# An FNet and GeGLU block on one core: chunk sums, weight chunks, first loads and last splits of the down projection moved in the instruction order

## The chip, the cores and the metric

The kernel runs on one core of one Trainium2 chip. The metric is the device time of one execution in microseconds (us), lower is better. Before the change it is 743.65 us, the median of 3 runs (743.02 to 745.65). The engines of the core are PE (TensorE, matrix products), DVE (VectorE), ACT (ScalarE), POOL (GpSimd) and SP (SyncE, which here only issues DMAs). Each engine, and SP's queue of DMAs, takes its instructions strictly in the order in which the program gives them.

## The reference

```python
def A(x, seq_re, seq_im, hid_re, hid_im):        # Fourier mixing as matrix products
    a = x @ hid_re.T ; b = x @ hid_im.T          # (2048, 448)
    return seq_re @ a - seq_im @ b
def B(x, w_gate, w_up, w_down):                  # GeGLU, 448 -> 1792 -> 448
    return (gelu_tanh(x @ w_gate) * (x @ w_up)) @ w_down
h  = x + A(layernorm(x), ...)
h2 = h + B(layernorm(h), ...)                    # float32 in and out, 2048 rows
```

## The kernel before

All products run on PE in float16, each operand split into a high half (`hi_part`, an ACT copy) and a low half (`lo_part`, a DVE subtraction), so that three products of halves give nearly float32. GeGLU's three products use Strassen-like forms: seven products of sums of blocks in place of eight. The sums of the down projection's operand are made on POOL, and one small one on DVE.

The order of every engine is written out by hand (`manual_schedule`); a step waits only for the data and buffers that it names.

**DFT.** Steps n = 0 to 63 (`N_STEPS`) multiply sequence blocks. Beside them DVE and ACT split the blocks (`seq_hi`, `seq_lo`) and some of the 14 gate/up weight chunks: class `Weights` loads a chunk's raw form (two DMAs, tile `gu_raw`), makes its sums (`sums`, four DVE operations into `gu_s`), its halves (`split`, into `gu_w`), and stores it to DRAM (`w_dram`). Table `DFT_F` says which chunk is done at which step: six chunks; the other eight (`JIT_F`, chunks 3 to 10) are done during the next stage, two units ahead of their use.

**Gate and up, first block of rows.** Units t = 0 to 13, one chunk of 128 hidden columns each, 512 rows wide. A unit is a `GateUp` with PE steps x1, z1, y1, x2, z2, y2, y3, where x1 and z1 of unit t+1 stand before y1 of unit t+1 and y3 of unit t. Step y2 ends in a DVE write to tile `hs`, `c_last` in a GELU on ACT and a product on POOL, y3 in a second DVE write to `hs`; then `hs` is stored to DRAM (`hid_dram`). The same units prepare the seven down-weight chunks n (`down_sums` on POOL, `down_hi`, `down_lo`), two of them in unit 0, then one a unit (`PREPS`). After units 0 and 1 come the last two hidden-DFT products (`hid_mm(7, 0)`, `hid_mm(7, 1)`), both into one PSUM bank of pool `ps_tr`, and added to the residual on DVE (`hid_add`).

**Gate and up, other blocks, with the down projection.** Units t = 14 to 41, half as wide. In each unit one or two chunks d of the down projection run too (`COUNT`, 42 chunks; `dn_mm`, 21 matmuls each). A chunk is loaded from `hid_dram` (`hid_load`), summed (`dn_sums`), split (`dn_hi`, `dn_lo`) and multiplied. Every seventh chunk ends a row block p: `Drain` adds its products to the residual, on DVE from PSUM, and on POOL in 8 operations spread over the two units that follow. Chunks of the last two row blocks (d = 42 to 55, `LAST`) can only be multiplied at the end; `EARLY` says in which unit (30 to 41) the first twelve are prepared, straight from tile `hs`, in the unit after it is complete.

**Tail.** `prev.y3()` of unit 41, then chunks 42 to 55 on PE, with the last two chunks' splits, the drains and the stores.

Of the kernel before, what the change touches and what calls it, by code (L numbers as in the profile page):

```python
# [13 lines left out]
P = 128  # L14
# [18 lines left out]
def kernel(  # L33
# [673 lines left out]
    def hid_mm(p, g):  # L707

        y = ys[p, g] = ps_tr.tile([P, 512], F32, tag="tr", name=f"y_{p}_{g}")
        for k in range(7):  # L710
            for m, (lz, lw) in enumerate(((0, 0), (0, 1), (1, 0))):
                PE.matmul(  # L712
                    y[:, :D],
                    z[p][:, lz, k, g * P : (g + 1) * P],
                    wh[:, lw, k, :],
                    start=k == 0 and m == 0,
                    stop=k == 6 and m == 2,
                )
# [10 lines left out]
    DFT_F = ((13, 20), (12, 25), (11, 30), (0, 45), (1, 48), (2, 50))  # L729
    JIT_F = range(3, 11)  # L730
# [286 lines left out]
    def plus(dst, ps, other):  # L1017
# [4 lines left out]
        (b, n): dram.tile([P, 4 - 2 * b, 4, P], F32, name=f"hid_dram{b}_{n}") for b in range(2) for n in range(NC)  # L1022
    }

    class GateUp:
# [78 lines left out]
        def store(self):  # L1104

            k, n = divmod(self.f, NC)
            if self.block == 0:
                nc.sync.dma_start(
                    hid_dram[0, n][:, :, 2 * k : 2 * k + 2], hs[self.t].rearrange("p (n g) t -> p n g t", g=2)
                )  # L1110
            else:
                nc.sync.dma_start(hid_dram[1, n], hs[self.t].rearrange("p (n k) t -> p n k t", k=4))
# [8 lines left out]
    def hid_load(d):  # L1121
        p, n = divmod(d, NC)
        hid_in[d] = fpool.tile([P, 4, P], F32, tag="hid", bufs=4, name=f"hid{d}")
        nc.sync.dma_start(hid_in[d], hid_dram[p // 4, n][:, p % 4])

    def dn_hid(d):
        p, n = divmod(d, NC)
        if d in hid_in:
            return hid_in[d]
        return hs[2 * NF + 2 * n].rearrange("p (n k) t -> p n k t", k=4)[:, p % 2]  # L1130

    LAST = range(6 * NC, 8 * NC)
    EARLY = {2 * NF + 2 * n + 2 + k: (6 + k) * NC + n for n in range(6) for k in range(2)}

    def dn_places():
# [29 lines left out]
    def dn_sums(d):  # L1165
        t = dn_hid(d)
        if d in LAST:
            s = prep.tile([P, 5, P], F32, tag="s", name=f"dn_s{d}")
        else:
            s = late.tile([P, 5, P], F32, tag="dn_s", bufs=2, name=f"dn_s{d}")  # L1170
        dn_s[d] = s
        G.tensor_add(s[:, 0:2], t[:, 0:2], t[:, 2:4])  # L1172
        G.tensor_sub(s[:, 2:4], t[:, 1:4:2], t[:, 0:4:2])  # L1173
        V.tensor_add(s[:, 4], t[:, 0], t[:, 3])
# [100 lines left out]
    PREPS = {0: (0, 1), 1: (2,), 2: (3,), 3: (4,), 4: (5,), 5: (6,)}  # L1275
# [7 lines left out]
    for t in range(NF):  # L1283
# [13 lines left out]
        if t == NF - 1:  # L1297
            dn_sums(0)
# [27 lines left out]
        for n in PREPS.get(t, ()):  # L1326
            if n == 1:
                down_hi(n, 0)
                down_lo(n, 0)
            down_hi(n, 1)  # L1330
            for part in W_LO1:
                down_lo(n, 1, part)
            if n + 1 < NC:
                down_sums(n + 1)
# [27 lines left out]
        for n in PREPS.get(t, ()):  # L1362
            if 2 <= n and n + 2 < NC:
                down_load(n + 2)
# [11 lines left out]
    for t in range(NF, N_GU):  # L1376
# [4 lines left out]
        for d in steps.get(t + 2, []):  # L1381
# [8 lines left out]
        for d in ahead:  # L1390
            dn_sums(d)
# [29 lines left out]
        for d in ahead[1:]:  # L1421
            dn_lo(d)
        if extra is not None:
            dn_sums(extra)
# [5 lines left out]
        if NF < t <= 2 * NF and t % 2 == 0:  # L1430
# [104 lines left out]
```

## Time and profile before

| what | value |
|---|---|
| median of 3 runs (lowest to highest) | 743.65 us (743.02 to 745.65) |
| the profiled execution's own time | 745.72 us |
| its span, first to last instruction | 743.9 us |
| mean granted clock of TensorE | 0.991 |
| DVE busy | 519.4 us, 70% of the span |
| ACT busy | 354.7 us, 48% |
| POOL busy | 201.6 us, 27%, nearly all of it after 343 us |
| bytes moved by DMA | 149.46 MB |

The page sums each engine's busy time over the whole span. The stages differ in what limits them, so such sums say little by themselves: idle time of PE is to be looked for by place, in the timeline and the list of waits, where a row's square bracket gives the idle time ahead of it and the instruction whose end released it.

### The profile page before, as it was taken

The page shows a single profiled execution, that of the slowest core. Times are in us where ns is not written, and L with a number is a line of the kernel's source. Part 1 is how long each engine was busy: PE and PEld are TensorE (multiplying, and loading weights), DVE is VectorE, ACT ScalarE, POOL GpSimd, SP SyncE. Part 2 cuts the span into 40 slices and gives each one's busy share as a digit, 9 for nine tenths or more (in the row PEclk, how much of TensorE's full clock was granted, in tenths as well). Part 3 has the DMA queues.
Part 4 walks back from the last instruction along what each step waited for, and adds up shares of the span by engine and source line. Part 5 has one row for each costly group of instructions (what it writes and reads, how often), then busy time and mean ns, then how long its engine had stood idle before and what let it go on. Part 6 is the DMA issues. An engine that isn't in the chain of part 4 may idle for free.

```text
span 743.9 us, 13045 instructions
## 1 busy us (share of the span) xinstructions
PE 712.6 (96%) x4952; PEld 482.1 (65%) x4952; DVE 519.4 (70%) x1024; ACT 354.7 (48%) x656; POOL 201.6 (27%) x240
## 2 busy tenths in 40 slices
PE   9999999999999999999889799979999999989898
PEld 5555555555555557986334344449999999878788
DVE  7996546668356699996659995337767667878742
ACT  5875424254234355443437674435555545546430
POOL 0000000000000000001424312134474767787852
PEclk9999999999999999999999999989999999999999
DMA  7796729898949898455438688976797975646202
GB/s 260 253 241 196 189 26 293 151 324 183 270 121 251 179 250 267 126 140 155 133 118 282 226 273 208 221 239 193 224 308 257 270 248 178 219 167 208 112 1 75
DMA packets 112863, 149.46 MB, mean 201 GB/s; under 512 B 61600, under 2 KB 80160, under 8 KB 112800
## 3 DMA queue, kind: packets, MB, share of 16 engines
q1 hardware_dynamic: 112800, 148.63, 69.0%
q8 instruction: 38, 0.62, 0.4%
q14 instruction: 25, 0.20, 0.1%
HBM read 103.51 MB, written 31.20 MB: 181 GB/s over the span
## 4 chain that ended last, share of the span: by engine, by line
PE 31%; DVE 7%; POOL 5%; ACT 3%; issue 2%; DMA 2%; SPq 0%; DVEq 0%; ACTq 0%; POOLq 0%
PE acc_d L1214 11%; PE pY L1008 9%; PE pZ L1008 5%; PE pX L1008 5%; DVE gu_w L114 2%; POOL dn_s L1173 1%; POOL dn_s L1172 1%; POOL hr L970 1%; PE y L712 1%; POOL hs L1102 1%; ACT dn_w L108 1%; DVE dn_w L112 1%; DVE wd L114 1%; DMA hid<-hid_dram 1%; DMA gu_raw<-in_w_gu_dram 1%
## 5 line engine op out<-in xcount | busy, mean ns | idle before, releaser
L647 PE MATMUL acc<-xs,ws 128*128 128x448 f16 x1248 | 238.0, 352 | 0.0
L647 PEld LDWEIGHTS <-ws 128*128 128x128 f16 x1248 | 122.0, 98 | 114.1 <-DVE ws L114 0.2
L1008 PEld LDWEIGHTS <-gw 128*128 128x128 f16 x1209 | 118.9, 98 | 39.2 <-issue 14.7
L1214 PE MATMUL acc_d<-wd,dn_w 128*128 128x224 f16 x945 | 106.6, 260 | 1.5 <-DVE dn_w L112 1.2
L219 POOL TENSOR_TENSOR wd_s<-wd 128x448 f32<-128x448 f32 x7 | 8.2, 1171 | 355.3 <-DVE r_h L141 341.9
L1214 PEld LDWEIGHTS <-dn_w 128*128 128x128 f16 x945 | 91.1, 98 | 4.8 <-DVE dn_w L112 1.7
L1102 POOL TENSOR_TENSOR hs<-hs,c 128x256 f32<-128x256 f32 (+1 forms) x42 | 48.1, 1146 | 148.1 <-ACT c L1100 105.2
L1008 PE MATMUL pY<-hops,gw 128*128 128x256 f16 (+1 forms) x527 | 75.5, 287 | 8.0 <-ACT pY L1053 5.5
L1008 PEld LDWEIGHTS <-gu_w 128*128 128x128 f16 x429 | 42.1, 98 | 62.6 <-issue 14.1
L114 DVE SCALAR_TENSOR_TENSOR ws<-wr,ws 128x1024 f16<-128x1024 f32 (+2 forms) x66 | 75.0, 1141 | 10.3 <-ACT ws L108 10.3
L108 ACT ACTIVATE ws<-wr 128x1024 f16<-128x1024 f32 (+2 forms) x66 | 64.0, 981 | 24.8 <-DMA wr<-in_w_seq_dram 24.1
L712 PE MATMUL y<-wh,z 128*128 128x448 f16 x336 | 67.8, 359 | 2.4 <-DVE hx L722 2.4
L712 PEld LDWEIGHTS <-z 128*128 128x128 f16 x336 | 33.3, 99 | 33.8 <-issue 4.8
L1008 PE MATMUL pZ<-hops,gw 128*128 128x256 f16 (+1 forms) x341 | 50.9, 283 | 3.4 <-DVE c L1018 3.4
L112 DVE TENSOR_TENSOR dn_w<-dn_s,dn_w 128x640 f16<-128x640 f32 x45 | 45.9, 1020 | 8.6 <-ACT dn_w L108 8.5
L1008 PE MATMUL pX<-hops,gw 128*128 128x256 f16 (+1 forms) x341 | 51.4, 285 | 0.0
L1008 PE MATMUL pY<-hops,gu_w 128*128 128x512 f16 x187 | 44.7, 382 | 6.9 <-DVE hs L1018 5.9
L108 ACT ACTIVATE dn_w<-dn_s 128x640 f16<-128x640 f32 x45 | 33.0, 733 | 35.7 <-POOL dn_s L1173 25.7
L519 PEld LDWEIGHTS <-ws 128*128 128x128 f16 x504 | 48.3, 98 | 0.9
L1018 DVE SCALAR_TENSOR_TENSOR c<-pZ,u 128x256 f32<-128x256 f32 (+1 forms) x42 | 21.4, 509 | 34.5 <-PE pZ L1008 34.5
L1064 ACT ACTIVATE u<-pY 128x256 f32<-128x256 f32 (+1 forms) x42 | 18.9, 450 | 50.6 <-PE pY L1008 50.6
L970 POOL TENSOR_TENSOR hr<-hr,v 128x224 f32<-128x224 f32 x56 | 41.5, 767 | 1.7 <-ACT v L938 1.2
(156 smaller groups left out, 975.8 us busy)
## 6 DMA issues: line engine op xcount, KB each, us to landing
gw<-w_dram SPq DMA_DIRECT2D x31, 896.0 KB, 5.0
wr<-in_w_seq_dram SPq DMA_DIRECT2D x100, 256.0 KB, 4.7
w_dram<-gu_w SPq DMA_DIRECT2D x14, 896.0 KB, 5.0
gu_raw<-in_w_gu_dram SPq DMA_DIRECT2D x28, 384.0 KB, 5.8
hid_dram<-hs SPq DMA_DIRECT2D x21, 512.0 KB, 6.7
hid<-hid_dram SPq DMA_DIRECT2D x42, 256.0 KB, 5.7
wr<-in_w_seq_dram SPq DMA_DIRECT2D x14, 512.0 KB, 5.7
x<-in_x_dram SPq DMA_DIRECT2D x16, 224.0 KB, 4.3
```

Of the source, the lines that this page charges most:

```text
L108: A.activation(dst, src, AF.Copy, scale=scale)
L112: V.tensor_sub(dst, src, hi)
L114: V.scalar_tensor_tensor(dst, src, scale, hi, op0=ALU.mult, op1=ALU.subtract)
L519: PE.matmul(fast_sum(n, k), fast_a(n, i, lw, a), fast_b(j, lx, b), start=j == 0 and m == 0 and k % 2 == 0, stop=j == NT // 2 - 1 and m == ...
L647: PE.matmul(acc[key][:, :D], w[:, lw, block * P : (block + 1) * P], xs[c][:, lx, :], start=c == 0 and m == 0, stop=c == NT - 1 and m == 2,)
L712: PE.matmul(y[:, :D], z[p][:, lz, k, g * P : (g + 1) * P], wh[:, lw, k, :], start=k == 0 and m == 0, stop=k == 6 and m == 2,)
L970: op(x, x, m)
L1008: PE.matmul(ps, w[:, wl, wa + ws, :], ops[:, m + ms, :], start=first and n == 0, stop=last and n == len(terms) - 1, skip_group_check=True,)
L1018: V.scalar_tensor_tensor(dst, ps, SC, other, op0=ALU.mult, op1=ALU.add)
L1064: A.activation(self.u2, self.Y, AF.Copy, scale=SC)
L1102: G.tensor_mul(c22, c22, self.cols(self.c12))
L1214: PE.matmul(ps, w[:, la, a, :], wd[n][:, lb, b, :], start=n == 0 and m == 0 and opens, stop=n == NC - 1 and m == 2, skip_group_check=True,)
```

## The change

The function `dn_sums` for the chunks of unit t+2 moves from the head of unit t+1 to the end of unit t, and the loads and sums of `EARLY` chunks to one unit ahead of their halves. These chunks are now loaded from DRAM like the others, so that `hs` of the last block is stored too, and the ring of `hs` shrinks from 3 to 2 while that of `hid` grows from 4 to 6. `EARLY` keeps eight chunks; six are split in the tail. Four weight chunks (7 to 10) go from `JIT_F` to `DFT_F`, and three keep their place in the DFT in other steps. Chunks 0 to 2 of the down projection are loaded in unit 12 instead of 13. Down-weight chunk n is prepared wholly in unit n. `hid_mm(7, 1)` writes another PSUM bank.

```diff
 def hid_mm(p, g):
-    y = ys[p, g] = ps_tr.tile([P, 512], F32, tag="tr", name=f"y_{p}_{g}")
+    pool, tag = (ps_dn, "a3") if p == NP - 1 and g else (ps_tr, "tr")
+    y = ys[p, g] = pool.tile([P, 512], F32, tag=tag, name=f"y_{p}_{g}")
...
-DFT_F = ((13, 20), (12, 25), (11, 30), (0, 45), (1, 48), (2, 50))
-JIT_F = range(3, 11)
+DFT_F = ((13, 17), (12, 20), (11, 25), (10, 29), (9, 33), (8, 37), (7, 41), (0, 45), (1, 48), (2, 50))
+JIT_F = range(3, 7)
...
-            hs[self.t] = fpool.tile([P, 8, P], F32, tag="hs", bufs=3, name=f"hs_{self.name}")
+            hs[self.t] = fpool.tile([P, 8, P], F32, tag="hs", bufs=2, name=f"hs_{self.name}")
...
 def hid_load(d):
     p, n = divmod(d, NC)
-    hid_in[d] = fpool.tile([P, 4, P], F32, tag="hid", bufs=4, name=f"hid{d}")
-    nc.sync.dma_start(hid_in[d], hid_dram[p // 4, n][:, p % 4])
+    hid_in[d] = fpool.tile([P, 4, P], F32, tag="hid", bufs=6, name=f"hid{d}")
+    b = max(p // 2 - 1, 0)
+    nc.sync.dma_start(hid_in[d], hid_dram[b, n][:, p % 2 if b else p])
 def dn_hid(d):
-    if d in hid_in:
-        return hid_in[d]
-    return hs[2 * NF + 2 * n].rearrange("p (n k) t -> p n k t", k=4)[:, p % 2]
+    return hid_in[d]
-EARLY = {2 * NF + 2 * n + 2 + k: (6 + k) * NC + n for n in range(6) for k in range(2)}
+EARLY = dict(zip((32, 33, 35, 37, 38, 39, 40, 41), (42, 49, 43, 50, 44, 51, 45, 52)))
...
-PREPS = {0: (0, 1), 1: (2,), 2: (3,), 3: (4,), 4: (5,), 5: (6,)}
 for t in range(NF):
...
-        if t + 1 == NF:
+        if t + 2 == NF:
             for d in (0, 1, 2):
                 hid_load(d)
+        if t + 1 == NF:
             hr_load(0)
...
-        if t == NF - 1:
-            dn_sums(0)
         cur.y1()
...
-        for n in PREPS[t][:1] if t in PREPS else ():
-            down_hi(n, 0)
-            down_lo(n, 0)
+        if t < NC:
+            down_hi(t, 0)
+            down_lo(t, 0)
         cur.x2()
+        if t < NC:
+            down_hi(t, 1)
...
+        if t == NF - 2:
+            dn_sums(0)
+        if t == NF - 1:
+            dn_sums(1)
+            dn_sums(2)
...
 for t in range(NF, N_GU):
-        for d in steps.get(t + 2, []):
+        far = steps.get(t + 2, []) + ([EARLY[t + 1]] if t + 1 in EARLY else [])
+        far += [46] if t + 1 == N_GU else []
+        for d in far:
             hid_load(d)
...
         prev.y3()
-        for d in ahead:
-            dn_sums(d)
         cur.y1()
...
         for d in ahead[1:]:
             dn_lo(d)
+        for d in far:
+            dn_sums(d)
         if extra is not None:
-            dn_sums(extra)
             dn_hi(extra)
             dn_lo(extra)
         do(t, 3)
-        if NF < t <= 2 * NF and t % 2 == 0:
+        if NF < t and t % 2 == 0:
             before.store()
...
 prev.y3()
-dn_sums(48)
+hid_load(47)
+prev.store()
+jit = [46, 47, 48, 53, 54, 55]
 for i, d in enumerate(range(6 * NC, 7 * NC + 4)):
     dn_mm(d)
-    if i == 0:
-        dn_hi(48)
-        dn_lo(48)
-        dn_sums(55)
-        dn_hi(55)
-        dn_lo(55)
-    if i == 1:
+    if jit:
+        n = jit.pop(0)
+        dn_hi(n)
+        if jit:
+            dn_sums(jit[0])
+        dn_lo(n)
+        if len(jit) > 1:
+            hid_load(jit[1])
+    if i == 5:
         drain.sums(range(8))
         dn_store(5)
```

**SP, units 12 and 13** (`gw` is the weight chunk of two units later, `hid` a chunk of the down projection, `hops` the transposed rows of the next block). Before:

```order
L1116 DMA gw_4723<-w_dram_149 128x3584
L1108 DMA hid_dram_4_3682<-hs_4691 512x1x256
L305 DMA_TRANSPOSE hops_3923<-xs_1_4633 128x8x128
L305 DMA_TRANSPOSE hops_3923<-xs_1_4633 128x6x128
L305 DMA_TRANSPOSE hops_3923<-xs_1_4633 128x3x128
L1116 DMA gw_4788<-w_dram_156 128x3584
L1124 DMA hid_4790<-hid_dram_0_3678 128x512
L1124 DMA hid_4792<-hid_dram_1_3679 128x512
L1124 DMA hid_4794<-hid_dram_2_3680 128x512
L1225 DMA hr_4796<-h_dram_141 128x896
```

Now:

```order
L1117 DMA gw_4738<-w_dram_149 128x3584
L1126 DMA hid_4740<-hid_dram_0_3750 128x512
L1126 DMA hid_4742<-hid_dram_1_3751 128x512
L1126 DMA hid_4744<-hid_dram_2_3752 128x512
L1109 DMA hid_dram_4_3754<-hs_4706 512x1x256
L305 DMA_TRANSPOSE hops_3993<-xs_1_4648 128x8x128
L305 DMA_TRANSPOSE hops_3993<-xs_1_4648 128x6x128
L305 DMA_TRANSPOSE hops_3993<-xs_1_4648 128x3x128
L1117 DMA gw_4813<-w_dram_156 128x3584
L1224 DMA hr_4815<-h_dram_141 128x896
```

The three loads stand ahead of the three last transposes and of the store of unit 11, where they stood behind them.

**POOL, end of unit 38 to unit 39** (`dn_s` with a chunk's number are its sums, `hr4` the residual of row block 4 in its drain, `hs` with `c12` the product of `c_last`). Before:

```order
L1102 TENSOR_TENSOR hs_38_7674<-hs_38_7674,c12_38_7672 128x2x128
L1172 TENSOR_TENSOR dn_s46_7725<-hs_36_7430 128x256
L1173 TENSOR_TENSOR dn_s46_7725<-hs_36_7430 128x256
L970 TENSOR_TENSOR hr4_6917<-hr4_6917,v0_4_7570 128x224 x2
L970 TENSOR_TENSOR hr4_6917<-hr4_6917,v1_4_7571 128x224 x2
L1172 TENSOR_TENSOR dn_s38_7756<-hid38_7608 128x256
L1173 TENSOR_TENSOR dn_s38_7756<-hid38_7608 128x256
L1172 TENSOR_TENSOR dn_s39_7760<-hid39_7610 128x256
L1173 TENSOR_TENSOR dn_s39_7760<-hid39_7610 128x256
L1102 TENSOR_TENSOR hs_38_7674<-hs_38_7674,c12_39_7797 128x2x128
```

Now:

```order
L1103 TENSOR_TENSOR hs_38_7667<-hs_38_7667,c12_38_7665 128x2x128
L1171 TENSOR_TENSOR dn_s38_7718<-hid38_7603 128x256
L1172 TENSOR_TENSOR dn_s38_7718<-hid38_7603 128x256
L1171 TENSOR_TENSOR dn_s38_7718<-hid39_7605 128x256
L1172 TENSOR_TENSOR dn_s38_7718<-hid39_7605 128x256
L1171 TENSOR_TENSOR dn_s51_7725<-hid51_7607 128x256
L1172 TENSOR_TENSOR dn_s51_7725<-hid51_7607 128x256
L971 TENSOR_TENSOR hr4_6922<-hr4_6922,v0_4_7560 128x224 x2
L971 TENSOR_TENSOR hr4_6922<-hr4_6922,v1_4_7561 128x224 x2
L1103 TENSOR_TENSOR hs_38_7667<-hs_38_7667,c12_39_7791 128x2x128
```

The sums of the chunks multiplied in unit 40 now stand ahead of the drain. The sums of the early chunk (46 before, 51 now) belong to halves that followed at once, and now follow one unit later. Chunk 39's sums share a tile with chunk 38's.

**DVE, end of unit 41 and tail.** Before:

```order
L1174 TENSOR_TENSOR dn_s54_8066<-hs_38_7674 128x128
L112 TENSOR_TENSOR dn_w1_8070<-hs_38_7674,dn_w1_8070 128x256
L112 TENSOR_TENSOR dn_w1_8070<-dn_s54_8066,dn_w1_8070 128x640
L1087 SCALAR_TENSOR_TENSOR hs_40_7916<-pY_41_7950,g1_41_8004 128x2x128
L1174 TENSOR_TENSOR dn_s48_8081<-hs_40_7916 128x128
L112 TENSOR_TENSOR dn_w1_8070<-hs_40_7916,dn_w1_8070 128x256
L112 TENSOR_TENSOR dn_w1_8070<-dn_s48_8081,dn_w1_8070 128x640
L1174 TENSOR_TENSOR dn_s55_8114<-hs_40_7916 128x128
```

Now:

```order
L1173 TENSOR_TENSOR dn_s46_8064<-hid46_7975 128x128
L112 TENSOR_TENSOR dn_xs_7968<-hid52_7852,dn_xs_7968 128x256
L112 TENSOR_TENSOR dn_xs_7968<-dn_s52_7964,dn_xs_7968 128x640
L1088 SCALAR_TENSOR_TENSOR hs_40_7911<-pY_41_7945,g1_41_8002 128x2x128
L1173 TENSOR_TENSOR dn_s47_8109<-hid47_8078 128x128
L112 TENSOR_TENSOR dn_w46_8106<-hid46_7975,dn_w46_8106 128x256
L112 TENSOR_TENSOR dn_w46_8106<-dn_s46_8064,dn_w46_8106 128x640
L1173 TENSOR_TENSOR dn_s48_8141<-hid48_8115 128x128
L112 TENSOR_TENSOR dn_w47_8138<-hid47_8078,dn_w47_8138 128x256
L112 TENSOR_TENSOR dn_w47_8138<-dn_s47_8109,dn_w47_8138 128x640
L1173 TENSOR_TENSOR dn_s53_8173<-hid53_8147 128x128
L112 TENSOR_TENSOR dn_w48_8170<-hid48_8115,dn_w48_8170 128x256
```

Chunk 48, which needs the last write to `hs` (L1087, now L1088), was summed from `hs` at once; now it goes to DRAM and back first, and its DVE sum stands ahead of the low halves of chunk 47.

More of the change, by code (lines that the diff above doesn't have):

```diff
@@ L1021 @@
     hid_dram = {
-        (b, n): dram.tile([P, 4 - 2 * b, 4, P], F32, name=f"hid_dram{b}_{n}") for b in range(2) for n in range(NC)
+        (b, n): dram.tile([P, 2 if b else 4, 4, P], F32, name=f"hid_dram{b}_{n}") for b in range(3) for n in range(NC)
     }
@@ L1167, in dn_sums @@
         if d in LAST:
-            s = prep.tile([P, 5, P], F32, tag="s", name=f"dn_s{d}")
-        else:
-            s = late.tile([P, 5, P], F32, tag="dn_s", bufs=2, name=f"dn_s{d}")
+            spare.append(d)
+            s = fops.tile([P, 5, P], F32, tag=("xn", "tt")[len(spare) % 2], name=f"dn_s{d}")
+        elif d % 4 < 2:
+            s = late.tile([P, 5, P], F32, tag="dn_s", bufs=2, name=f"dn_s{d}")
+        else:
+            if d % 4 == 2:
+                opened["s"] = prep.tile([P, 10, P], F32, tag="s", name=f"dn_s{d}")
+            s = opened["s"][:, d % 4 % 2 * 5 :][:, :5]
         dn_s[d] = s
@@ L1325 @@
             gw[t + 2] = w.w
[L1326 to L1330, printed above, removed]
+        if t < NC:
             for part in W_LO1:
-                down_lo(n, 1, part)
-            if n + 1 < NC:
-                down_sums(n + 1)
+                down_lo(t, 1, part)
+            if t + 1 < NC:
+                down_sums(t + 1)
         if t == NF - 1:
@@ L1361 @@
             gu[t + 4] = Weights(t + 4)
-        for n in PREPS.get(t, ()):
-            if 2 <= n and n + 2 < NC:
-                down_load(n + 2)
+        if 1 <= t and t + 3 < NC:
+            down_load(t + 3)
         do(t, 4)
```

10 lines of the change are left out of this document (2 added, 8 removed).

## The prediction

> **What bounds the kernel now.** I read the page's busy times first, then who waited for whom on PE, then PE's timeline at those waits, then busy times and clock by stretch.
>
> ```profile
> PE 712.6 (96%) x4952; PEld 482.1 (65%) x4952; DVE 519.4 (70%) x1024; ACT 354.7 (48%) x656; POOL 201.6 (27%) x240
> PE pY L1008 <- ACT pY L1053: 6.5, 5, 2.2
> PE pY L1008 <- DVE hs L1018: 5.9, 3, 2.4
> PE pZ L1008 <- DVE c L1018: 3.4, 2, 3.1
> PE pZ L1008 <- ACT m L1059: 3.3, 1, 3.3
> PE y L712 <- DVE hx L722: 2.4, 1, 2.4
> ```
>
> PE is busy 712.6 of 743.9 us: the kernel is PE's instruction stream with about 31 us of holes. Matmuls aren't changed, so the change can win only holes, and lose by making new ones. The waits (us in total, times, longest) have no single culprit: ACT, DVE and, behind both, POOL and DMAs. The next view says where they lie (columns: stretch, its length, then busy time of PE, PEld, DVE, ACT, POOL with counts, granted clock, DMA share, GB/s).
>
> ```profile
> 83.00:228.00 145.00, 145.00 (x769) 74.99 (x767) 84.80 (x175) 51.22 (x81) 0.00 (x0) 1.00 0.78 201
> 345.90:434.90 89.00, 76.46 (x343) 33.96 (x341) 69.53 (x116) 49.15 (x85) 30.26 (x26) 0.96 0.60 191
> 487.60:502.00 14.40, 10.21 (x62) 6.93 (x61) 6.21 (x12) 5.07 (x12) 6.23 (x8) 0.76 0.67 242
> 640.00:714.20 74.20, 64.21 (x606) 58.27 (x605) 57.58 (x100) 36.87 (x89) 54.98 (x65) 1.00 0.41 144
> ```
>
> The DFT has no hole (145.00 of 145.00). Three stretches have: 12.5 us at units 0 to 8, 4.2 us at unit 14, 10.0 us at units 33 to 41. In two of them the clock is below 1, which costs more than the idle time:
>
> ```profile
> 363.20:366.60 3.40, 3.02 (x8) 1.06 (x8) 3.37 (x5) 2.58 (x6) 2.00 (x2) 0.50 0.04 14
> 376.80:380.20 3.40, 3.40 (x11) 1.36 (x10) 0.51 (x2) 0.00 (x0) 2.09 (x3) 0.50 0.94 346
> 492.90:499.70 6.80, 5.90 (x24) 3.59 (x25) 3.20 (x5) 1.56 (x6) 4.05 (x5) 0.50 0.33 113
> ```
>
> After three of the holes PE ran at half clock for 3.02, 3.40 and 5.90 us of busy time: 12.32 us that should take half, 6.2 us lost.
>
> **Units 0 to 8.** The holes, from PE's timeline (start, length, [idle before it and what ended it]):
>
> ```profile
> 363.58 2.29 PE L1008 MATMUL pZ<-hops,gu_w 128*128 128x512 f16 x5 [3.26 <-ACT m L1059]
> 376.52 5.82 PE L712 MATMUL y<-wh,z 128*128 128x448 f16 x21 [2.38 <-DVE hx L722]
> 400.95 2.53 PE L1008 MATMUL pY<-hops,gu_w 128*128 128x512 f16 x11 [1.56 <-DVE hs L1018]
> 411.92 2.53 PE L1008 MATMUL pY<-hops,gu_w 128*128 128x512 f16 x11 [2.39 <-DVE hs L1018]
> 422.40 2.53 PE L1008 MATMUL pY<-hops,gu_w 128*128 128x512 f16 x11 [1.91 <-DVE hs L1018]
> ```
>
> The first is unit 1's z2. ACT had the copy `m` queued behind the high half of down-weight chunk 1, and that waited for POOL:
>
> ```profile
> ACT wd L108 <- POOL wd_s L222: 4.2, 1, 4.2
> ```
>
> Chunks 0 and 1 were both prepared in unit 0. Now chunk 1's halves stand in unit 1, behind x2, a PE unit later than its sums: the 3.26 us go. The second hole is `hid_mm(7, 1)` waiting for its bank until DVE added `hid_mm(7, 0)`; with a bank of its own nothing is left to wait for: 2.38 us go. Both half-clock stretches behind them go too: (3.02 + 3.40) / 2 = 3.2 us.
>
> The next three are units 3, 4 and 5, where DVE makes a weight chunk (5, 6, 7) and a down chunk beside the unit's own work. Chunk 7 leaves unit 5, so the 1.91 us go. Chunks 5 and 6 stay JIT and the down chunks stay at one a unit, so I keep 1.56 and 2.39. What a chunk costs DVE:
>
> ```profile
> L114 DVE SCALAR_TENSOR_TENSOR gu_w<-gu_s,gu_w x28: 677/686/1764, 114.4 to 446.9; 128x512 f16<-128x512 f32 x28
> L328 DVE TENSOR_TENSOR gu_s<-gu_raw x14: 540/552/1165, 103.5 to 441.6; 128x384 f32<-128x384 f32 x14
> L330 DVE TENSOR_TENSOR gu_s<-gu_raw x14: 414/419/878, 104.6 to 442.6; 128x256 f32<-128x256 f32 x14
> ```
>
> Four sums (two like each of the last rows, 1.9 us) and low halves of 14 blocks (the first row's 0.69 us covers four, so 2.4): 4.3 us. The four chunks that leave took DVE 17 us here, but chunks 8 to 10 stood where PE hardly waited, so only one hole goes with them.
>
> One hole costs a little more than its bracket, since matmuls overlap: a row's length reaches past the start of the next one.
>
> ```profile
> 669.48 1.36 PE L1008 MATMUL pY<-hops,gw 128*128 128x256 f16 x11
> 670.68 0.71 PE L1008 MATMUL pX<-hops,gw 128*128 128x256 f16 x5
> ```
>
> 669.48 + 1.36 - 670.68 = 0.16 us, lost at every stop. Units 0 to 8 give 3.26 + 2.38 + 1.91 + 3.2 + 3 x 0.16 = **11.2 us**.
>
> On the clock: the Trainium skill, TensorE: Matmul & The Clock Gate (Why this matters for your kernels), wants idle gaps between bursts of matmuls kept under about 3 us, since a longer one brings the half clock. The rows here agree at 3.26 us and not at 2.38 us, which also halved the clock, while 2.39 us at 411.92 did not. By the page the two holes that I keep leave the clock alone; by the row at 376.52 one of them could cost 1.7 us more. Those 1.7 us stand in my range, since the rows differ.
>
> **Four chunks in the DFT.** DVE is busy 84.8 of the 145 us from step 17 to 44; 17 us more make 102. PE doesn't wait for it as long as the splits of the sequence blocks stay ahead, and their loads wait for free buffers, so they run ahead of need:
>
> ```profile
> SPq L432 <- DVE ws L114: 20.6, 8, 5.8
> gu_raw<-in_w_gu_dram SPq DMA_DIRECT2D x28, 384.0 KB, 5.8
> w_dram<-gu_w SPq DMA_DIRECT2D x14, 896.0 KB, 5.0
> hid_dram<-hs SPq DMA_DIRECT2D x21, 512.0 KB, 6.7
> ```
>
> Per chunk two raw loads and a store, 1.66 MB; four are 6.7 MB on top of 145 x 201 GB/s = 29 MB, so the DMA share of 0.78 becomes 0.96. I take **0**, between 0 and the unhidden time of the rivals below.
>
> **Unit 14.** DVE stood at the first chunk's sums until its load landed, and c, which z1 of unit 14 needs, stood behind; the three loads had been issued behind three transposes that kept SP's queue for 7.96 us.
>
> ```profile
> 491.51 0.82 PE L1008 MATMUL pZ<-hops,gw 128*128 128x256 f16 x6 [3.08 <-DVE c L1018]
> 493.80 0.93 PE L1214 MATMUL acc_d<-wd,dn_w 128*128 128x224 f16 x4 [0.95 <-DVE dn_w L112]
> 490.56 0.29 DVE L1174 TENSOR_TENSOR dn_s<-hid 128x128 f32<-128x128 f32 x1 [6.74 <-DMA hid<-hid_dram]
> 475.99 7.96 SPq L305 DMA_TRANSPOSE hops<-xs  x3
> 484.63 1.67 SPq L1124 DMA_DIRECT2D hid<-hid_dram  x3
> DMA to landing us min/median/max: 4.3/5.7/8.6
> ```
>
> The last row is the `hid` loads'. Issued ahead of the transposes, at about 475, they land by 476.6 + 8.6 = 485.2 even at the longest, ahead of unit 14's first matmul (487.6); DVE's first sum, now at the end of unit 12, may stand for it with nothing urgent behind. So the two stops go, and half of 5.90: 3.08 + 0.95 + 2.95 + 2 x 0.16 = **7.3 us**. Queued behind the loads now are the transposes, 1.67 us later, their issue over at 485.6; the first matmuls that need them are y1 of unit 14, at about 489 and later. With two `hs` buffers the write in y2 of unit 14 (at about 493.6 without the stops) waits for the store of unit 12, issued at about 486 and landed 6.7 us later by the row above: even, and a microsecond late would only hold DVE, not PE. I charge nothing for both.
>
> **Units 33 to 41.** Behind PE's stops on ACT's copies stand ACT's stops on POOL's sums; halves of an early chunk were queued right behind its sums.
>
> ```profile
> ACT dn_w L108 <- POOL dn_s L1173: 25.7, 18, 3.1
> L970 POOL TENSOR_TENSOR hr<-hr,v 128x224 f32<-128x224 f32 x56 | 41.5, 767 | 1.7 <-ACT v L938 1.2
> L1173 POOL TENSOR_TENSOR dn_s<-hid x42: 719/773/1387, 491.4 to 701.4; 128x256 f32<-128x256 f32 x42
> 714.19 2.46 PE L1214 MATMUL acc_d<-wd,hops 128*128 128x224 f16 x24 [1.37 <-DVE hs L1087]
> ```
>
> Now early sums come a unit ahead of their halves, and ordinary sums ahead of the drain's four POOL operations (4 x 0.77 = 3.1 us) instead of behind them. (For ordinary chunks that is all: they are loaded in the same unit as before, so the sums can't start sooner than the landing.) Four early chunks also leave for the tail, 4 x 2 x 0.77 = 6 us less on POOL. Of the stretch's 10.0 us idle I keep the 1.37 at its end, since DVE's queue ahead of L1087 is as long as before: 8.6 us in some eleven stops, with 11 x 0.16 it is 10.4. Against it stands DVE: its small sum now waits for the landing ahead of y3's write, and in units 32 and 39 three such sums and an early chunk's low halves come together, some 3 us in a unit of 6. Between 0 and 6 us, I take 2: **8.4 us**. For units 14 to 30, without early chunks, I charge **0.3**.
>
> **The tail.** Chunk 48 now goes y3, store, load, sums, halves. With the shortest landings 3.3 (the shortest `hid_dram` store) + 4.3 + two POOL sums 1.45 + ACT 0.73 + DVE 0.82 = 10.6 us after 714.14; with medians (6.7, 5.7) 15.4. PE reaches it five chunks of 2.01 and 0.3 us after 714.19, 10.4. So it waits 0.2 to 5.0 us; few DMAs run then, so nearer the lower: **1.0**.
>
> **The sum**, on the profiled execution's 745.72: 11.2 + 7.3 + 8.4 - 0.3 - 1.0 = 25.6, so 720.1. The median of the runs is 2.07 lower; I subtract from it: 743.65 - 25.6 = **718 us**.
>
> **Rivals.** (a) Half of it: the down stage stays bound by landings and DVE, because ordinary sums gain nothing from their new place, and chunk 48 waits its 5 us: 8.4 shrinks to 4 and the tail costs 4 more, 726; if unit 14 also still stops long enough for the half clock, 730. For it speak DVE's 57.6 of 74.2 us and the median landings; against it that units 14 to 30 run with the same chain and no holes. (b) Slower: the DFT becomes bound by DMA. A share of 0.22 is free and the four chunks need 0.18 of it; it turns when the transposes, which hold SP's queue while they are issued, leave less than that usable. Then the added 6.7 MB show, at worst all of them at 201 GB/s, 33 us: 743.65 - 25.6 + 33 = 751. Against it: loads wait for buffers today, and PE has no hole to show. (c) Not what it says: the holes are DVE's own total work, and move on by a unit; then only the two certain ones of unit 1 go, with the clock: 734. DVE's 69.5 of 89.0 us speaks against it.
>
> **How the numbers follow.** Forecast 718 with its own range 712 to 725: 0.66. Rival (a), 725 to 731: 0.20; (c), to 740: 0.06; (b): 0.04; below 711, if the kept holes (3.95) and the allowances (3.3) go too: 0.04. The range of 711 to 731 holds the first two. A measurement of this kernel tells about 0.5% (3.7 us) from no change: faster by more 0.94, within 0.02, slower 0.04.
>
> **What would show it.** Right: no hole over 1 us in units 1, 2, 5 and 14, the clock at 1.00 from 5 us to the end, holes left of about 1.6 and 2.4 us in units 3 and 4, and of 1 to 1.5 us ahead of L1088 of unit 41; DFT's PE still full. Wrong: PE stops before 346 us; stops of `dn_mm` on `dn_w` in units 33 and 40; a stop over 3 us at chunk 48, or the last store waiting for POOL's drains.

## The result, and the profile after

The changed kernel takes 733.17 us (median of four runs, 732.43 to 733.44), beside 744.6 us of the kernel before in the same comparison: a ratio of 0.985 with a 95% interval of 0.982 to 0.987. The forecast was 718 us with a range of 711 to 731. The direction was right; under half of the gain came. The profiled execution took 733.34 us, span 730.6.

Busy times, waits of PE (us in total, times, longest) and the stretches of the prediction, moved by what PE had gained by then. Columns of the last five rows as before: stretch, length, busy time of PE, PEld, DVE, ACT, POOL, granted clock, DMA share, GB/s:

```profile
PE 709.9 (97%) x4952; PEld 483.5 (66%) x4952; DVE 527.6 (72%) x1024; ACT 355.6 (49%) x656; POOL 207.6 (28%) x240
PE acc_d L1213 <- ACT v L939: 7.0, 2, 6.3
PE pY L1009 <- DVE hs L1019: 4.5, 2, 2.9
PE acc_d L1213 <- DVE hs L1088: 2.0, 1, 2.0
PE pZ L1009 <- DVE c L1019: 1.5, 2, 1.3
...
83.00:228.00 145.00, 145.00 (x768) 74.97 (x767) 96.00 (x200) 55.25 (x91) 0.00 (x0) 1.00 0.87 237
345.90:425.60 79.70, 74.44 (x343) 33.65 (x342) 58.96 (x96) 44.92 (x76) 32.77 (x26) 0.98 0.61 190
478.30:485.10 6.80, 6.80 (x62) 5.81 (x61) 5.29 (x8) 4.71 (x12) 4.75 (x5) 1.00 0.97 316
623.60:689.80 66.20, 62.87 (x611) 58.90 (x610) 61.40 (x97) 35.46 (x84) 54.44 (x63) 1.00 0.69 237
689.80:727.20 37.40, 31.10 (x276) 29.14 (x275) 18.78 (x32) 6.11 (x11) 19.06 (x26) 0.86 0.21 74
```

The list of waits has a new head: `PE acc_d <- ACT v`, one wait of 6.3 us that before did not have. Four of the five stretches did what was forecast or nearly; the last, the tail, now has 6.3 us without a matmul and a clock of 0.86. The holes of over an idle microsecond in PE's timeline from unit 4 on:

```profile
403.43 4.22 PE L1009 MATMUL pY<-hops,gu_w 128*128 128x512 f16 x11 [2.94 <-DVE hs L1019]
625.72 0.82 PE L1009 MATMUL pZ<-hops,gw 128*128 128x256 f16 x6 [1.30 <-DVE c L1019]
689.79 3.95 PE L1213 MATMUL acc_d<-wd,hops 128*128 128x224 f16 x24 [2.03 <-DVE hs L1088]
712.00 0.72 PE L1213 MATMUL acc_d<-wd,hops 128*128 128x224 f16 x3 [6.30 <-ACT v L939]
```

Behind three of them the clock was halved. The last two rows are 3.40 + 5.90 us of PE's time, of which half, 4.65 us, was lost in the last unit and the tail:

```profile
403.80:407.20 3.40, 3.40 (x10) 1.22 (x8) 2.68 (x5) 0.64 (x2) 3.40 (x2) 0.51 0.57 226
690.60:694.00 3.40, 3.40 (x21) 2.78 (x19) 1.36 (x2) 0.74 (x1) 0.34 (x1) 0.50 0.42 159
711.00:717.90 6.90, 5.90 (x33) 4.82 (x32) 0.00 (x0) 1.09 (x2) 6.56 (x11) 0.51 0.17 66
```

Where the time went is read from the start of the same matmul in both timelines (the first x1 matmul of a unit, which is issued at the end of the unit before; the first matmul of chunk 42, behind which PE waits for the last y3; and the last matmul of all). The rows are cut where the terms of the forecast end:

| stretch | forecast, us | measured, us |
|---|---|---|
| up to x1 of unit 0 (four chunks in the DFT) | 0 | +0.06 |
| from there to x1 of unit 14 | -11.2 | -9.39 |
| to x1 of unit 15 | -7.3 | -7.57 |
| to x1 of unit 34 | +0.3 | +1.02 |
| to the first matmul of chunk 42, at 710.94 before and 685.87 now | -8.4 | -9.19 |
| to the last matmul of all (the wait for the last y3, and the tail) | +1.0 | **+11.63** |
| sum | -25.6 | -13.44 |

The profiled times differ by 12.38 us only, since 2.7 us of this one lie outside its span and 1.8 of the one before.

Up to chunk 42 the change gained 25.07 us of the 26.6 forecast; the last row lost almost half of that again. It has a stop that costs 6.47 us (6.30 idle and the overlap), 0.67 us more at the last unit's y3 (2.20 for 1.53) and 4.65 us of half clock, in sum 11.8. What ended the 6.30 us stands in the timelines of POOL and ACT:

```profile
697.27 0.83 POOL L1171 TENSOR_TENSOR dn_s<-hid 128x256 f32<-128x256 f32 x1 [6.33 <-DMA hid<-hid_dram]
...
706.31 11.33 POOL L971 TENSOR_TENSOR hr<-hr,v 128x224 f32<-128x224 f32 x16
...
711.41 0.54 ACT L939 ACTIVATE v<-acc_d 128x448 f32<-128x448 f32 x1 [4.29 <-POOL hr L971]
```

POOL stood 6.33 us waiting for chunk 48's load, did the sums of 48, 53, 54 and 55, and only then row block 5's eight operations, which the change had moved from `i == 1` to `i == 5`. They read the tiles `v0` and `v1`, of which there is one each. So ACT, copying row block 6's banks into the same tiles, waited 4.29 us for POOL, and PE, whose next product goes into a bank that row block 6 still held, waited for ACT.

### The profile page after: what moved, and what is told of

It is laid out like the page before. It is cut to its first block, busy times and chain, and to the rows that moved or that the text cites. A ratio compares the mean times of both kernels' runs of the same rounds, so it can differ in the third digit from the quotient of the medians.

```text
span 730.6 us, 13052 instructions
## 1 busy us (share of the span) xinstructions
PE 709.9 (97%) x4952; PEld 483.5 (66%) x4952; DVE 527.6 (72%) x1024; ACT 355.6 (49%) x656; POOL 207.6 (28%) x240
## 4 chain that ended last, share of the span: by engine, by line
PE 83%; DVE 7%; POOL 4%; DMA 3%; ACT 2%; issue 1%; SPq 0%; DVEq 0%; POOLq 0%; ACTq 0%
PE acc L647 32%; PE pY L1009 12%; PE acc_d L1213 11%; PE y L713 9%; PE pZ L1009 7%; PE pX L1009 7%; PE acc_f L519 6%; DMA hid<-hid_dram 2%; POOL hr L971 2%; DVE dn_w L112 1%; DVE gu_w L114 1%; POOL dn_s L1171 1%; POOL dn_s L1172 1%; DMA hid_dram<-hs 1%; DMA wr<-in_w_seq_dram 1%
## 5 line engine op out<-in xcount | busy, mean ns | idle before, releaser
L1009 PEld LDWEIGHTS <-gw 128*128 128x128 f16 x1365 | 133.3, 98 | 44.8 <-issue 1.9
L1213 PEld LDWEIGHTS <-dn_w 128*128 128x128 f16 x1008 | 96.9, 98 | 2.8 <-issue 0.9
L1009 PE MATMUL pY<-hops,gw 128*128 128x256 f16 (+1 forms) x595 | 89.2, 294 | 0.0
L1103 POOL TENSOR_TENSOR hs<-hs,c 128x256 f32<-128x256 f32 (+1 forms) x42 | 52.8, 1257 | 126.5 <-DVE hs L1019 69.1
L1009 PE MATMUL pZ<-hops,gw 128*128 128x256 f16 (+1 forms) x385 | 61.7, 294 | 1.5 <-DVE c L1019 1.5
L1009 PE MATMUL pX<-hops,gw 128*128 128x256 f16 (+1 forms) x385 | 61.7, 294 | 0.0
L1171 POOL TENSOR_TENSOR dn_s<-hid 128x256 f32<-128x256 f32 x56 | 48.2, 861 | 34.9 <-DMA hid<-hid_dram 31.8
L112 DVE TENSOR_TENSOR dn_w<-dn_s,dn_w 128x640 f16<-128x640 f32 x48 | 54.1, 1127 | 0.1
L1009 PEld LDWEIGHTS <-gu_w 128*128 128x128 f16 x273 | 27.0, 99 | 38.9 <-issue 8.6
L1173 DVE TENSOR_TENSOR dn_s<-hid 128x128 f32<-128x128 f32 x56 | 30.8, 565 | 27.1 <-DMA hid<-hid_dram 26.8
L1172 POOL TENSOR_TENSOR dn_s<-hid 128x256 f32<-128x256 f32 x56 | 45.1, 806 | 0.0
```

The costliest lines, as they stand in the source:

```text
L112: V.tensor_sub(dst, src, hi)
L1009: PE.matmul(ps, w[:, wl, wa + ws, :], ops[:, m + ms, :], start=first and n == 0, stop=last and n == len(terms) - 1, skip_group_check=True,)
L1103: G.tensor_mul(c22, c22, self.cols(self.c12))
L1213: PE.matmul(ps, w[:, la, a, :], wd[n][:, lb, b, :], start=n == 0 and m == 0 and opens, stop=n == NC - 1 and m == 2, skip_group_check=True,)
```

## The experiments

Theory A: row block 5's drain, held back behind the six splits, holds `v0` and `v1`, and through ACT's copies stops PE. Theory B, the rival: the six splits themselves queue ahead of the copies. All edits are to the changed kernel; times are those of one profiled run each unless a median is given. Single runs of the kernel before, taken beside them, read 745.02 us in one batch (the first four experiments) and 742.57 in the other (the next four), so a difference of 2 to 3 us between two single totals says little by itself.

**The drain, moved forward.**

```diff
-        if i == 5:
+        if i == 0:
             drain.sums(range(8))
             dn_store(5)
```

> Edit: row block 5's eight POOL operations and its store stand behind the sums of chunk 47 (i == 0) instead of behind those of chunk 55 (i == 5). Theory A (held drain: the tiles v0 and v1 stay with row block 5 until POOL is through, so ACT can't copy row block 6's banks and PE's product 7 of chunk 49 waits for its bank): POOL does them in its idle 6.3 us from about 691 to 696.5; what is left is ACT's high halves of chunks 54 and 55, which stand ahead of the copies until about 707.1, so PE's idle time ahead of L1213 at 705.7 falls from 6.30 to 2 to 2.5 us and the half clock behind it from 6.8 to at most 3.4 us: 4 to 7 us less, 726 to 729. Theory B (it is the six splits themselves, ACT and DVE having too much ahead of the copies): the copies come no sooner, the stop stays over 5 us, 732 to 734.

727.28 us. Row block 5's operations fill POOL's idle time, and the stop falls to 2.28 us with no half clock behind it:

```profile
691.71 5.85 POOL L971 TENSOR_TENSOR hr<-hr,v 128x224 f32<-128x224 f32 x8
```
```profile
709.77 0.45 PE L1213 MATMUL acc_d<-wd,hops 128*128 128x224 f16 x3 [2.28 <-ACT v L939]
```

Three small stops on low halves of chunks 47 and 48 (0.43, 1.18 and 0.52 us) are new. DVE's small sum of the next chunk, which waits for that chunk's load, stands ahead of these halves; and the load of 53 now stands in SP's queue behind the store of row block 5.

**The tiles alone.**

```diff
+        if p == 6:
+            both = prep.tile([P, 10, P], F32, tag="s", name="v_6").rearrange("p o t -> p (o t)")
+            v = [both[:, k * D : (k + 1) * D] for k in range(2)]
```

> Edit: only the two copies of row block 6 get memory of their own (the tile of the sums, free by then); row block 5's POOL operations stay at i == 5. Theory A: ACT's wait of 4.29 us for POOL goes, the copies start at about 707.1 and PE's stop falls from 6.30 to 2 to 2.5 us, though row block 5's drain is as late as in the changed kernel: 726 to 729, as with the drain moved. Theory B: as before, 732 to 734. If the late drain counts by itself (its store, or POOL's 16 operations in a row ahead of the last additions) and not through the tiles, the stop goes and the end stays at 733.

726.04 us, and the same 2.28 us stop, though POOL does row block 5 as late as in the changed kernel (16 operations from 707.18 on). ACT's copies start at once behind the halves of chunk 55:

```profile
707.89 0.96 ACT L939 ACTIVATE v<-acc_d 128x448 f32<-128x448 f32 x2
```
```profile
708.47 0.45 PE L1213 MATMUL acc_d<-wd,hops 128*128 128x224 f16 x3 [2.28 <-ACT v L939]
```

The half clock behind unit 4 and behind the last unit's y3 is there in this run as in the changed kernel (it begins at 403.83 and 690.55 us here, at 403.84 and 690.56 there), so what its span lost, 6.3 us (730.6 to 724.3), is the tail's alone. It is the tiles through which the late drain acts, as A says, and not its store or POOL's 11 us in a row.

**Chunk 55's halves alone, behind the copies.**

```diff
-        if jit:
+        if len(jit) > 1:
             n = jit.pop(0)
...
             drain.bank3()
+            dn_hi(55)
+            dn_lo(55)
             drain.sums(range(8))
```

> Edit: only the halves of chunk 55 (two ACT copies, two DVE subtractions) stand behind the copies and bank additions of row block 6 instead of ahead of them; row block 5's drain stays at i == 5. Theory A: the copies wait for POOL as before, until about 711, so the stop stays at 6 us and the time within 1 us of the changed kernel: 732 to 734. Theory B: the copies come at about 705 and the stop shrinks to under 1 us: 723 to 726.

The stop stays, and ACT waits longer for POOL instead of for its own queue. B as the only cause falls; it may still have a share that shows once the tiles are free:

```profile
708.60 0.54 ACT L939 ACTIVATE v<-acc_d 128x448 f32<-128x448 f32 x1 [6.09 <-POOL hr L971]
```
```profile
709.19 0.72 PE L1213 MATMUL acc_d<-wd,hops 128*128 128x224 f16 x3 [6.04 <-ACT v L939]
```

The time is 729.51 us all the same, below the expectation. 3.4 us of the difference is the half clock behind unit 4 and behind the last unit's y3, which this run didn't have, at places that the edit doesn't touch (see the last section). From here on stops are compared, and totals only where they differ by more than that.

**Both, and chunk 54 in a buffer that doesn't wait for chunk 48** (`i == 0`, the edit above, and):

```diff
-        elif d % 5 < 3:
+        elif d % 5 < 3 or d == 54:
```

> Edit: both of these, and chunk 54's halves in a buffer that doesn't wait for chunk 48's matmuls. Theory A with what it leaves to ACT: no stop over 0.5 us behind chunk 48 and no half clock there, 6.3 + 3.4 us less: 723 to 724.5, with the stop of 2.0 us at 689.8 and its half clock still there. Theory B: as the kernel with chunk 55 alone moved.

723.35 us. The 21 matmuls of chunk 49 now run in one piece, where the changed kernel had 18, the stop, and 3:

```profile
704.11 2.18 PE L1213 MATMUL acc_d<-wd,hops 128*128 128x224 f16 x21
```

The half clock behind unit 4 and the last y3 is there again (from 403.55 and 690.27). A's link takes some 4 us of the stop, the halves of 54 and 55 ahead of the copies the other 2 (so B had a share; the two edits to these halves were not tried apart), and the tail's half clock goes with them.

**The drain back at its old number.**

```diff
-        if i == 5:
+        if i == 1:
```

> Edit: row block 5's drain back where the kernel before had it, at i == 1, which is now behind the sums of chunk 48. Theory A with POOL's order: those sums can't start before chunk 48's load has landed (about 697), so the drain takes 699 to 704.5 and pushes the sums of 53, 54 and 55 and with them the halves of 55 to about 712, ahead of the copies: the stop behind chunk 48 stays at 5 to 7 us with its half clock, 731 to 735. If only the eight operations' place behind all six splits counted, it would give 726 to 729.

734.1 us; the stop is even longer, and longer than the 5 to 7 us expected:

```profile
698.32 6.37 POOL L971 TENSOR_TENSOR hr<-hr,v 128x224 f32<-128x224 f32 x8
```
```profile
713.84 0.72 PE L1213 MATMUL acc_d<-wd,hops 128*128 128x224 f16 x3 [8.93 <-ACT v L939]
```

The drain at `i == 1` stands behind the sums of chunk 48, which wait for the load, and ahead of those of 53 to 55, on which ACT then waits ahead of its copies. For 2.38 us of it POOL stands at the sums of 54, whose load was issued at 705.16, behind the store of row block 5. It isn't the number of the step that counts but which side of the waiting sums the drain stands on.

**The last unit's y3 ahead of the halves of chunk 52.**

```diff
         if t + 1 < N_GU:
             cur.z1()
+        else:
+            prev.y3()
...
-    prev.y3()
     hid_load(47)
```

> Edit: the last unit's y3 (its DVE write frees the bank of row block 6's product 7) is called ahead of the sums of chunk 46 and the halves of chunk 52; PE's order stays. Theory: the write comes at about 686.8 instead of 689.3, the stop of 2.03 us at L1213 behind 687.5 goes (under 0.3 us) and with it the half clock of 690.6 to 694.0; the tail's stop of 6.3 us stays, its half clock too. 3 to 4 us less: 729 to 730.5. Rival (the write waits for PE or POOL, not for DVE's queue): no change, 733.

The stop is gone; the matmuls that it had cut run in one piece:

```profile
684.29 4.19 PE L1213 MATMUL acc_d<-wd,hops 128*128 128x224 f16 x42
```

727.01 us, about 2 us below the expectation: unit 4's half clock (1.7 us) was missing in this run too. The tail's stop was 6.48 us.

**Unit 4 without a chunk of down.**

```diff
+    PREP = {0: 0, 1: 1, 2: 2, 3: 3, 5: 4, 6: 5, 7: 6}
...
-        if t < NC:
-            down_hi(t, 0)
-            down_lo(t, 0)
+        if t in PREP:
+            down_hi(PREP[t], 0)
+            down_lo(PREP[t], 0)
```

> Edit: unit 4 gets no chunk of down; chunks 4, 5 and 6 are made in units 5, 6 and 7. Unit 3 keeps its chunk. Theory (DVE has a weight chunk and a down chunk in the same unit): the stop of unit 4 (3.1 us lost at 400) goes or falls under 0.7 us, and the half clock behind it; unit 3's 1.7 us stays: 4 to 5 us less, 728.5 to 729.5. Rival (the weight chunk alone is what makes DVE late): 2 us or more of the stop stay, 731 to 733.

728.57 us. Of the 3.11 us lost in unit 4 there are 0.30 left, and 0.55 are new in unit 7; unit 3's stop is unchanged, as it should be:

```profile
391.89 2.53 PE L1009 MATMUL pY<-hops,gu_w 128*128 128x512 f16 x11 [1.56 <-DVE hs L1019]
```

A weight chunk and a down chunk in one unit are what makes DVE late there, not the weight chunk alone.

**DVE's small sum behind the next unit's y3.** In the changed kernel DVE waited in that sum for the load, with the halves of an early chunk and then y3 and c queued behind it:

```profile
622.58 0.29 DVE L1173 TENSOR_TENSOR dn_s<-hid 128x128 f32<-128x128 f32 x1 [1.33 <-DMA hid<-hid_dram]
```

```diff
-        V.tensor_add(s[:, 4], t[:, 0], t[:, 3])
+            later.append(d)
...
         prev.y3()
+        for d in later:
+            V.tensor_add(dn_s[d][:, 4], dn_hid(d)[:, 0], dn_hid(d)[:, 3])
```

> Edit: in the down stage DVE's one sum of a chunk stands behind the next unit's y3 write instead of at the end of the unit, where DVE waits in it for the load to land. Theory: the stops in units 23, 24 (0.40 and 0.89 us lost) and 33 (1.47 us) go: 2 to 2.7 us less, 730.5 to 731.5, and DVE's waits for hid (26.8 us, 22 times) fall below 10 us outside the tail. Rival (those stops are DVE's own work, not its waits): they stay within 0.3 us, 733.

731.65 us. Half of it held. The stop of 1.30 us ahead of unit 34's z1 (in the loop's unit 33) falls to under 0.3 us, and DVE's waits in this sum in the down stage (485 to 690 us) from 20.3 us (first row, changed kernel) to 6.1 us (second row), with 0.5 us more at the one chunk that kept its old place. But the stop at the head of unit 24 (0.72 us idle in the changed kernel) didn't go; it grew to 2.19 us and brought the half clock:

```profile
DVE dn_s L1173 <- DMA hid<-hid_dram: 20.3, 20, 2.5
```
```profile
DVE dn_s L1180 <- DMA hid<-hid_dram: 6.1, 6, 1.9
```
```profile
545.26 0.83 POOL L1171 TENSOR_TENSOR dn_s<-hid 128x256 f32<-128x256 f32 x1 [2.58 <-DMA hid<-hid_dram]
...
546.86 0.74 ACT L108 ACTIVATE dn_w<-dn_s 128x640 f16<-128x640 f32 x1 [1.23 <-POOL dn_s L1172]
...
550.92 0.74 PE L1220 MATMUL acc_d<-wd,dn_w 128*128 128x224 f16 x6 [2.19 <-ACT v L939]
```

There it is ACT that stands in a high half, waiting for POOL's sums of the same load, with row block 1's copies behind it: there the landing itself is late, whoever waits for it (POOL's wait for it was 2.55 us in the changed kernel). The total is no proof of a gain: the half clock behind unit 4 and the last y3, 3.4 us, is missing in this run.

**All together**, first without that last edit, with row block 5's store only at `i == 3`, behind the loads of 53 to 55:

> Edit: the three that helped together: row block 5's drain behind the sums of 47 (its store only at i == 3, behind the loads of 53 to 55), chunk 54 in a buffer that doesn't wait for chunk 48 and chunk 55's halves behind row block 6's copies; the last unit's y3 ahead of chunk 46's sums; chunks 4 to 6 of down a unit later. Theory (the three stops are independent and their gains add): 9.8 + 3.9 + 4.6 less than the changed kernel: 714 to 717, no stop over 0.7 us behind 640 us and the clock full from unit 5 to the end. Rival (a gain is given back: with PE earlier at chunk 48, whose load is no earlier, it waits there): a stop of 1 to 4 us at chunk 48 or 53, 718 to 721.

720.22 us, the median of five (717.4 to 720.93), ratio to before 0.966 (0.964 to 0.968), above the expectation. The three stops went, but the rival has part of it. With y3 earlier POOL has only some 3 us to spare (688.43 to the landing at about 691.5) ahead of chunk 48's sums, and the drain takes 6.48; ACT and PE wait for these sums, and the stops came close enough together to halve the clock once more:

```profile
688.43 6.48 POOL L971 TENSOR_TENSOR hr<-hr,v 128x224 f32<-128x224 f32 x8
...
696.55 0.74 ACT L108 ACTIVATE dn_w<-dn_s 128x640 f16<-128x640 f32 x1 [4.58 <-POOL dn_s L1172]
...
697.35 0.37 PE L1213 MATMUL acc_d<-wd,dn_w 128*128 128x224 f16 x2 [0.80 <-ACT dn_w L108]
```

Next, with DVE's small sums moved as above:

> Edit: the same with DVE's small sums behind the next unit's y3. Theory: the stop of unit 33 (1.3 to 1.7 us) goes, that of units 23 and 24 stays as ACT's wait for POOL's sums and so for the landing: 0.5 to 1.5 us less than without: 713 to 716.

716.69 us, the median of four (715.95 to 717.18), ratio 0.9625 (0.961 to 0.964), 0.7 us above the expected time. That is 3.5 us less than without this edit, where 0.5 to 1.5 was expected; 1.7 us of half clock in the other kernel's profiled execution is part of the difference. PE is busy for 99% of the span, and the mean clock is 1.000, with no slice of the 40 below 90%:

```profile
PE 704.4 (99%) x4952; PEld 479.7 (67%) x4952; DVE 524.3 (73%) x1024; ACT 355.6 (50%) x656; POOL 206.3 (29%) x240
...
PEclk9999999999999999999999999999999999999999
```

Last, row block 6's copies in memory of their own and the drain of row block 5 in two halves:

```diff
+        if i == 0:
+            drain.sums(range(4))
+        if i == 4:
+            drain.sums(range(4, 8))
+            dn_store(5)
```

> Edit: as the kernel with all edits, but row block 6's copies get memory of their own, and of row block 5's eight POOL operations four stand behind the sums of chunk 47 and four (with the store) behind those of chunk 55. Theory (with y3 earlier POOL's idle time ahead of chunk 48's sums is only about 4 us, and eight operations of 5.9 to 6.5 us there make those sums late, which is what the stops on chunk 48's halves are): four operations, 2.9 us, fit; the stops of 0.45 and 0.49 us on chunks 47 and 48 fall below 0.3 us in sum, or only the first stays, which waits for the landing of chunk 48's load: 715.5 to 716.5. Rival (those stops come from DVE's queue): as before, 716 to 717.5.

716.73 us, the median of five (715.4 to 718.25), ratio 0.964 (0.961 to 0.966): no gain. Chunk 48's sums no longer wait for the drain, only for the load; yet stops of 0.52 and 0.27 us on chunks 47 and 48 stay, 0.79 in sum where under 0.3 was expected. The first comes from DVE's queue, as the rival had it: DVE stands 3.71 us in the small sum of chunk 48, with chunk 47's low half behind it.

```profile
691.04 0.29 DVE L1174 TENSOR_TENSOR dn_s<-hid 128x128 f32<-128x128 f32 x1 [3.71 <-DMA hid<-hid_dram]
```
```profile
693.52 2.19 PE L1220 MATMUL acc_d<-wd,dn_w 128*128 128x224 f16 x21 [0.52 <-DVE dn_w L112]
```

The last two versions are alike, faster than both kernels, and within 1.3 us of what was forecast for the change; but they get there in part by taking away stops that the forecast kept (in unit 4 and at the last y3).

**The changed kernel once more.**

> No edit: the changed kernel once more. Theory on the clock (it is set in steps of 3.41 us on a grid that doesn't start with the program, and a step is halved when PE stood still for over about 2.1 us of the step before): the stop of 3.11 us in unit 4 is there again with the same length, but the half clock behind it only if 2.1 us of it or more fall in one step; the stop of 2.0 to 2.2 us in the last unit halves the clock only if nearly all of it falls in one; the 6.3 us stop always fills one step, so 3.4 us or more of half clock are there again. 731 to 734.

730.2 us, below the expectation and 3.1 us less than the other profiled execution of the same program. The large stops are nearly the same (2.94 us in unit 4, 2.04 at y3, 6.69 in the tail), but half clock follows only the last of them. PE, not slowed by half clock at y3 here, also stands 0.52 us at chunk 47 and 0.27 at chunk 48.

## Why the prediction failed

The time lies in the range of rival (c), 731 to 740, but not by its mechanism: (c) had the holes move on by a unit, with only those of unit 1 gone. The holes of units 5 and 14 went too, and most of those of units 34 to 41.

**The DFT: 0, right.** +0.06 us; its 145 us are full, with DVE at 96.0 us (102 forecast) and a DMA share of 0.87 (0.96 forecast). Rival (b) fell.

**Units 0 to 13: the steps right, unit 4 mis-sized.** Unit 1's z2 gave 4.89 us with its half clock, the bank of `hid_mm(7, 1)` 4.22 (2.38 + 1.70 + 0.16 forecast), unit 5 2.07 (1.91 + 0.16), and a small stop of unit 6, not in the forecast, 0.46. The hole kept in unit 4 was not 2.39 us but 2.94, and it brought the half clock, the 1.7 us that the prediction left to its range: +2.24 us. The run without a down chunk in unit 4 shows that the pair of chunks makes this stop; why it grew by 0.55 us was not tried.

**Unit 14: right**, 7.57 us for 7.3; PE has no hole and no half clock there.

**Units 15 to 33: 1.02 us lost for 0.3.** It is all at unit 24: 0.4 us ahead of its z1, where DVE's small sum waits for the landing ahead of y3's write, and 0.9 behind it, where ACT's copies stand behind late sums; a stop of 0.26 us went.

**Units 34 to 41: right**, 9.19 us for 8.4. The prediction named the mechanism against the gain (DVE's small sum waits for the landing ahead of y3's write) and put 2 us on it; it cost 1.47, ahead of unit 34's z1. The other stops of this stretch went.

**The tail: this step failed.** The prediction put it as "So it waits 0.2 to 5.0 us; few DMAs run then, so nearer the lower: **1.0**". Measured in its place: +11.63 us with the last y3, most of it a stop of 6.30 us behind chunk 48 and the half clock after it. The prediction followed one chain, chunk 48's store, load, sums and halves, and had that nearly right: in this execution chunk 48 didn't stop PE, though with some luck, since the half clock at y3 brought PE to it 1.7 us later; in the second execution chunks 47 and 48 cost 0.79 us idle. But the diff moved a second thing, the eight POOL operations and the store of row block 5, and the working gave them neither time nor a reader. Their 6 us (5.85 where they run early) were nothing in themselves: POOL had stood idle for 6.33. What they held was `v0` and `v1`. The prediction had asked this very question for the store ("the last store waiting for POOL's drains" stood among the signs), not for the tiles. Missed with it: product 7 of row block 7 takes a bank of row block 6, and that bank is read by the copies that now came last. Freeing the tiles alone takes 4.0 us off the stop, as moving the drain alone does, so this link is shown from two sides; the rest of the stop is the halves of chunks 54 and 55 ahead of the copies, which the prediction didn't price either. With the drain moved and these halves out of the way the stop is gone and 9.0 us of the span with it (730.6 to 721.6; 10 us of the time).

**The end of the last unit: mis-sized.** The kept 1.37 us became 2.03 us and halved the clock, 0.67 + 1.7 us. Moving y3's write ahead of chunk 52's halves took the stop away; why it had grown from 1.37 us was not tried.

## What to carry to other kernels

When operations move behind a waiting instruction, price what they hold, not only what they take: list each tile that they are the last to read, who writes it next, and who waits for that. An engine that idles for a load is the place for work that frees buffers: put it ahead of the operation that waits for the load, and only as much as fits. And where a kernel has stops of 2 to 3 us, compare kernels by the stops of their profiles before their times, because the clock adds or leaves out some microseconds from run to run.

## What the runs showed of the clock

The half clock is given out in steps. In the changed kernel the three half-clock stretches begin at 403.84, 690.56 and 711.04 us: 84 and 6 times 3.413 us apart. Before had them at 363.16, 376.81 and 492.86: 4 and 34 times. Where the grid lies against the kernel differs from run to run, and each step's clock follows, with two exceptions below, from how busy PE was in the step before. Steps of four kernels by the same view (the first busy time is PE's; the clock is the third number from the right); first the changed kernel, unit 4 and then the last unit:

```profile
400.42:403.83 3.41, 0.47 (x3) 0.19 (x2) 3.41 (x7) 1.92 (x4) 0.31 (x1) 1.00 0.40 136
403.84:407.25 3.41, 3.41 (x9) 1.22 (x8) 2.64 (x5) 0.60 (x2) 3.41 (x2) 0.50 0.60 233
687.14:690.55 3.41, 1.38 (x15) 1.22 (x13) 3.41 (x6) 1.40 (x4) 2.65 (x4) 1.00 0.01 4
690.56:693.97 3.41, 3.41 (x21) 2.79 (x19) 1.40 (x2) 0.74 (x1) 0.38 (x1) 0.50 0.42 159
```

the kernel with chunk 55 moved, unit 4:

```profile
397.53:400.94 3.41, 2.35 (x11) 0.98 (x10) 3.38 (x8) 2.40 (x3) 0.21 (x1) 1.00 0.78 280
400.94:404.35 3.41, 1.53 (x8) 0.70 (x8) 3.41 (x7) 1.63 (x3) 1.44 (x1) 1.00 0.06 21
404.35:407.76 3.41, 3.41 (x17) 1.55 (x16) 2.74 (x4) 1.62 (x3) 3.41 (x3) 1.00 0.93 282
```

the kernel with the drain moved forward, the stop of 2.28 us in the tail:

```profile
706.06:709.47 3.41, 1.43 (x15) 1.27 (x14) 3.38 (x6) 2.01 (x5) 1.70 (x3) 1.00 0.02 5
709.47:712.88 3.41, 3.11 (x33) 3.11 (x33) 2.18 (x6) 0.68 (x2) 3.01 (x5) 1.00 0.00 0
```

and the kernel before, the stops of 2.38 and then of 2.39 us:

```profile
373.40:376.80 3.40, 1.02 (x6) 0.41 (x5) 2.47 (x5) 1.59 (x3) 0.74 (x1) 1.00 0.75 234
407.53:410.94 3.41, 2.00 (x10) 0.78 (x8) 3.38 (x8) 1.26 (x2) 0.00 (x0) 1.00 1.00 384
410.94:414.35 3.41, 2.43 (x12) 1.13 (x12) 2.98 (x5) 2.65 (x4) 2.19 (x1) 1.00 0.52 196
```

The same stop of 2.94 us lies in one step in the changed kernel (0.47 us busy, half clock next) and is cut in two in the kernel with chunk 55 moved (2.35 and 1.53, full clock). A full-clock step with 1.38 us of PE time or less was followed by half clock in all those looked at, one with 1.43 us or more by full clock, but for two: one of the 723.35 us kernel (1.45 us, from 686.85) and one of the 720.22 us kernel (1.69 us, from 695.63), both followed by half clock. So the border is not sharp, and PE's busy time may not be quite what sets it. Unit 4's stop is in nine profiles, 2.93 to 2.94 us long: half clock behind it in four, none in five. This also accounts for the two rows of the prediction that seemed to differ: before, the stop of 2.38 us fell into one step and the one of 2.39 us into two. No kernel was made to shift the grid; the reading rests on these profiles.

The Trainium skill, TensorE: Matmul & The Clock Gate (What's actually happening), has a window of 3413 ns that runs free of the kernel's start; the 3.413 us here agree. Its advice to keep gaps under about 3 us (Why this matters for your kernels) is no safe bound here: 2.03 us halved the clock.
